# Top-k attention and a leaky MLP: the reciprocal one round later, scores before the split, weight loads from ScalarE, last chunks merged

## The chip, the core and the metric

The kernel runs on one core of a Trainium2 chip. A core has five engines with a queue each: TensorE (PE, matrix products, with PEld for its weight loads), VectorE (DVE), ScalarE (ACT), GpSimd (POOL) and SyncE (SP), which here gives out nearly all transfers. The metric is device time in microseconds, the median of several runs; lower is better.

## The reference

For 8 batches and 8 heads, 576 queries look at 576 keys of 64 elements. Of each row of scores the 32 largest are kept, a softmax is taken over them, and the values are weighed. The result, 4608 tokens of 512, goes through an MLP with a leaky activation.

```python
scores = scale * np.matmul(q, k.transpose(0, 1, 3, 2))
kth = np.partition(scores, -top_k, axis=-1)[..., -top_k:-top_k + 1]
mask = scores >= kth
scores = np.where(mask, scores, -1000000000.0)
scores = scores - np.max(scores, axis=-1, keepdims=True)
attn = np.exp(scores)
attn = attn / (np.sum(attn, axis=-1, keepdims=True) + 1e-09)
return np.matmul(attn, v).astype(np.float32)
# x = that, as 4608 x 512
h = x @ w_in                       # 512 x 2048
g = np.maximum(0.01 * h, h)
return (g @ w_out).astype(np.float32)
```

The MLP weights arrive as 64-bit floats, which the kernel turns into 32-bit ones by itself.

## The kernel before

The work is cut into 144 units, each 128 query rows of two heads. A software pipeline handles one unit per step: in step s VectorE finds the top 32 of unit s in four rounds of eight, GpSimd masks unit s-1, ScalarE exponentiates and normalizes unit s-2 and splits it into 16-bit halves for a transpose by DMA, and in every second step TensorE makes the scores of two units ahead and weighs the values of two units behind. Between these parts lie seven portions of MLP work. The engines' queues get the instructions in this order:

```python
for s in range(len(steps) + LAG + 1):
    cur, old = unit(s), unit(s - 1)
    older, oldest, new = unit(s - 2), unit(s - LAG), ()
    ...                              # every second step: new = two units ahead
    picks = top_k(cur) if cur else iter(())
    budget = slot_budget(s)

    def slot(n):
        next(picks, None)            # one top-k round
        if s in gap and n:
            convert()                # in steps 4 to 9: weights instead
    slot(0)
    if old:
        mask(old, 0); mask(old, 1)
    if older:
        exponents(older, 0); exponents(older, 1)
        sums(older)
    mlp_steps(budget)
    mlp_steps(budget)
    slot(1)
    if older:
        reciprocals(older)
    mlp_steps(budget)
    if older:
        normalize(older, 0); normalize(older, 1)
    slot(2)
    mlp_steps(budget)
    if older:
        transpose(older)
    mlp_steps(budget)
    slot(3)
    for u in new[:1]:
        scores(u)
    if s % 2 == 0:
        for u in (unit(s - LAG - 1), oldest):
            if u: weigh_values(u)
    for u in new[1:]:
        scores(u)
    mlp_steps(budget)
    mlp_steps(budget)
    ...
```

The parts that the change touches:

```python
def scores(u):                       # one PSUM buffer for both heads (psc0, psc1)
    ps = [ps_sc.tile([P, 2, 512], F32, name=f"psc{i}") for i in range(2)]
    ...                              # matmuls
    for i in range(2):
        nc.scalar.copy(u.s[i]..., ps[i][:, :, 0:HS])

def sums(u):
    nc.scalar.activation(u.ze, u.z, AF.Copy, bias=1e-9, scale=1.0)
def reciprocals(u):
    nc.vector.reciprocal(u.rz, u.ze)
def normalize(u, i):
    nc.scalar.activation(u.s[i], u.s[i], AF.Copy, bias=0.0, scale=u.rz[:, i:i + 1])

def transpose(u):
    for h in range(2):
        split = work.tile([P, 2 * S], U16, name="split", bufs=2)
        nc.scalar.copy(split, pairs[:, :, h])
        nc.sync.dma_start(apart[:, h, :], split)
    nc.sync.dma_start_transpose(out=u.wT..., in_=apart...)
```

The weights come in 16 chunks of 1 MB as 64-bit words, into three buffers (`raws`). In each slot 1 to 3 of the steps 4 to 9 (`gap`), the conversion begun two slots ago is finished on VectorE, the next is begun, and another load is given out:

```python
def convert_weights(dst, raw, on_vector):
    nc.vector.tensor_scalar(ex, hi, ...)          # begin: exponent and mantissa
    nc.vector.tensor_scalar(man, hi, ...)
    if on_vector:                                 # even chunks, counted from 0
        nc.vector.tensor_scalar(ex, ex, ...)
        nc.scalar.activation(ex, ex, ...)
    else:                                         # odd chunks
        nc.scalar.activation(exf, ex, ...)        # three on ScalarE
        ...
    nc.scalar.activation(frac, lo, ...)           # frac lies in raw
    yield
    nc.vector.scalar_tensor_tensor(out=dst, in0=man, ..., in1=frac, ...)   # finish
    nc.vector.scalar_tensor_tensor(out=ex, in0=hi, ...)                    # last to read raw
    nc.vector.tensor_tensor(dst, dst, exf, ALU.mult)

def convert():
    if len(converting) == 2 or not raw_chunks:
        for c in converting[:1]:
            next(converting.pop(0), None)
    if raw_chunks:
        begun[0] += 1
        converting.append(convert_weights(*raw_chunks.pop(0), on_vector=begun[0] % 2 == 1))
        next(converting[-1])
    fetch_weights()
```

The MLP takes tokens in chunks, numbered from 0. A chunk can begin once the values of all its tokens are weighed; its work is spread evenly over the steps until the next chunk is ready. Two chunks of 128 tokens, sixteen of 256 and two of 128 make the 4608.

```python
def mlp(ch):
    n = CHUNKS[ch]
    for f in range(NFC):                          # 16
        for c in range(HP):                       # 4
            nc.tensor.matmul(ph[:, 0:n], w_in[c][...], x[c][:, 0:n], ...)
            ...
        nc.scalar.activation(gT[f][:, 0:n], ph[:, 0:n], AF.Prelu, alpha=SLOPE)
        ...
    for r0 in range(0, n, P):
        for f in range(NFC):
            nc.tensor.matmul(pz[0:m, 0:DMODEL], gT[f][:, r0:r0 + m], w_out..., ...)
            ...
        nc.scalar.copy(o_sb[0:m], pz[0:m, 0:DMODEL])
        nc.sync.dma_start(out[...], o_sb[0:m])

def slot_budget(s):
    after = [at for at, _ in ready_at if at >= s]
    until = gap[-1] if s in gap else after[0] if after else s
    return backlog[0] / ((until + 1 - s) * SLOTS)
```

Of the kernel before, what the change touches and what calls it, by code (L numbers as in the profile page):

```python
# [17 lines left out]
def kernel(  # L18
# [13 lines left out]
    nc = tc.nc  # L32
# [13 lines left out]
    WCH = 1024  # L46
    LEFT = S % P
    assert D == 64 and S == 576 and HP == 4 and B % 2 == 0 and LEFT == 64
    CHUNKS = [128] * 2 + [256] * 16 + [128] * 2
    assert sum(CHUNKS) == B * S  # L50
    CHMAX = max(CHUNKS)
    LOADED, LOADED_V = 5, 5
# [31 lines left out]
            yield (w_out[f // 4][:, f % 4:f % 4 + 2, :],  # L84
                   moe_w_out[f * P:(f + 2) * P, :].rearrange("(g p) n -> p g n", g=2))

    def load_weights(dst, src):

        if src.dtype == F32:
            nc.sync.dma_start(dst, src)  # L90
            return None
        raw = raws.tile([P, WCH, 2], U32, name="raw")
        to = raw.rearrange("p n w -> p (n w)")
        if len(src.shape) == 3:
            dst = dst.rearrange("p g n -> p (g n)")
            to = to.rearrange("p (g n) -> p g n", g=2)
        nc.sync.dma_start(to, src)
        return dst, raw

    def convert_weights(dst, raw, on_vector):  # L100
# [29 lines left out]
    def load_qk(pi):  # L130
        qt = loads.tile([P, S], F32, name="qt")
        kt = loads.tile([P, S], F32, name="kt")
        nc.sync.dma_start(qt, qT[pi])
        nc.sync.dma_start(kt, kT[pi])
        qk_of[pi] = qt, kt

    def load_v(pi):
        v_of[pi] = loads.tile([P, NKC, 2, D], F32, name="vt", bufs=LOADED_V)
        nc.sync.dma_start(v_of[pi], vk[pi])
# [28 lines left out]
    def scores(u):  # L168
        ps = [ps_sc.tile([P, 2, 512], F32, name=f"psc{i}") for i in range(2)]
        for n in range(0, len(u.parts), 2):  # L170
            for half in range(2):
                for i, pi, side, r0 in u.parts[n:n + 2]:
                    qt, kt = qk_of[pi]
                    d = slice(side * D, (side + 1) * D)
                    nc.tensor.matmul(  # L175
                        ps[i][r0:r0 + u.rows, half, 0:HS],
                        qt[d, u.q0:u.q0 + u.rows],
                        kt[d, half * HS:(half + 1) * HS],
                        start=True, stop=True,
                    )  # L180
        u.both = work.tile([P, 2, S], F32, name="s_sb", bufs=5)
        u.s = [u.both[:, i, :] for i in range(2)]
        for i in range(2):
            nc.scalar.copy(u.s[i].rearrange("p (h n) -> p h n", h=2), ps[i][:, :, 0:HS])  # L184

    def top_k(u):

        u.tops = small.tile([P, 2, ROUNDS, 8], F32, name="tops")
        rest = [work.tile([P, S], F32, name=f"rest{i}", bufs=1) for i in range(2)]
        src = u.s  # L190
        for r in range(ROUNDS):
            for i in range(2):
                nc.vector.max(out=u.tops[:, i, r, :], in_=src[i])  # L193
            if r + 1 < ROUNDS:
                for i in range(2):
                    nc.vector.match_replace(out=rest[i], in_to_replace=u.tops[:, i, r, :],  # L196
                                            in_values=src[i], imm_value=LOWEST)
                src = rest
            yield
# [42 lines left out]
    def x_at(token):  # L242

        c = 0
        while token >= CHUNKS[c]:
            token -= CHUNKS[c]
            c += 1
# [21 lines left out]
    def mlp(ch):  # L269

        n = CHUNKS[ch]
        t0 = sum(CHUNKS[:ch])
        x = x_of[ch]
        for f in range(NFC):
            ph = ps_ml.tile([P, 512], F32, name="ph", tag="ml")
            for c in range(HP):
                nc.tensor.matmul(  # L277
                    ph[:, 0:n], w_in[c][:, f * P:(f + 1) * P], x[c][:, 0:n],
                    start=(c == 0), stop=(c == HP - 1),
                )  # L280
                if c == 1:
                    yield 2 * max(n, 225)
            nc.scalar.activation(gT[f][:, 0:n], ph[:, 0:n], AF.Prelu, alpha=SLOPE)  # L283
            yield 2 * max(n, 225)
        for r0 in range(0, n, P):
            m = min(P, n - r0)
            pz = ps_ml.tile([P, 512], F32, name="pz", tag="ml")
            for f in range(NFC):
                nc.tensor.matmul(  # L289
                    pz[0:m, 0:DMODEL], gT[f][:, r0:r0 + m], w_out[f // 4][:, f % 4, :],  # L290
                    start=(f == 0), stop=(f == NFC - 1),
                )
                if f % 2 and f + 1 < NFC:
                    yield 2 * DMODEL
            o_sb = work.tile([P, DMODEL], F32, name="o_sb", bufs=1)
            nc.scalar.copy(o_sb[0:m], pz[0:m, 0:DMODEL])  # L296
            nc.sync.dma_start(out[t0 + r0:t0 + r0 + m, :], o_sb[0:m])
            yield 2 * DMODEL
# [8 lines left out]
    def mlp_steps(budget):  # L307
        owed[0] += budget
        while owed[0] > 0:
            if running[0] is None:  # L310
                if not ready:
                    owed[0] = 0.0
                    return
                running[0] = mlp(ready.pop(0))
            cost = next(running[0], None)
            if cost is None:
                running[0] = None
            else:
                owed[0] -= cost
                backlog[0] -= cost  # L320
# [14 lines left out]
    def unit(n):  # L335
        return steps[n] if 0 <= n < len(steps) else None
# [25 lines left out]

    chunks, raw_chunks = weight_chunks(), []

    def fetch_weights():
        chunk = next(chunks, None)
        got = load_weights(*chunk) if chunk else None
        if got:
            raw_chunks.append(got)

# [6 lines that stand above are left out]
            begun[0] += 1  # L377
            converting.append(convert_weights(*raw_chunks.pop(0), on_vector=begun[0] % 2 == 1))
            next(converting[-1])
        fetch_weights()  # L380

    with tc.manual_schedule():
        last = {p: n for n, u in enumerate(steps) if u for p in u.pairs}
        for p in range(HP):
            load_qk(p)
            if p < 2:
                scores(units[p])
        for _ in range(3):
            fetch_weights()
        for p in range(HP):  # L390
            load_v(p)

        def load_more(s):

            for of, load, n, lag in ((qk_of, load_qk, LOADED, -2), (v_of, load_v, LOADED_V, LAG + 1)):
                while len(of) < NPAIR and (len(of) < n or last[len(of) - n] + lag <= s):
                    load(len(of))
# [4 lines that stand above are left out]
            if s % 2 == 0 and s not in gap:  # L402
                ahead = units if s < FIRST else steps
                new = ahead[s + 2:s + 4]
# [4 lines that stand above are left out]
                next(picks, None)  # L409
                if s in gap and n:  # L410
                    convert()

            slot(0)
            if old:
                mask(old, 0)
                mask(old, 1)
            if older:
                exponents(older, 0)
                exponents(older, 1)
                sums(older)  # L420
            mlp_steps(budget)
            mlp_steps(budget)
            slot(1)
            if older:
                reciprocals(older)
            mlp_steps(budget)
            if older:
                normalize(older, 0)
                normalize(older, 1)
            slot(2)  # L430
            mlp_steps(budget)
            if older:
                transpose(older)
            mlp_steps(budget)
            slot(3)
            for u in new[:1]:
                scores(u)
            if s % 2 == 0:
                for u in (unit(s - LAG - 1), oldest):
                    if u:  # L440
                        weigh_values(u)
# [4 lines that stand above are left out]
            attended(s)  # L446
            if s >= gap[-1]:
                load_more(s)
        mlp_steps(1e9)
# [53 lines left out]
```

## Time and profile before

The median of 3 runs is 1656.01 us (1655.76 to 1659.07); the profiled execution spans 1656.4 us.

| stretch (us) | what happens | VectorE busy | TensorE busy | ScalarE busy |
|---|---|---|---|---|
| 45 to 142 | weights are converted | 86.88 | 39.09 | 66.36 |
| 142 to 290 | top-k; few tokens for the MLP yet | 144.94 | 93.16 | 90.64 |
| 290 to 410 | steady state begins | 111.90 | 114.11 | 86.20 |
| 410 to 1520 | steady state | 1057.47 | 1052.45 | 796.31 |
| 1520 to 1593 | last top-k rounds | 48.90 | 71.00 | 40.00 |
| 1593 to 1656 | last values and MLP | 1.28 | 57.49 | 20.07 |

In the profile's lines, a group or instruction is named by line of the kernel, engine and operation, with output and input. Line 193 is the maximum of a top-k round, 196 its replacement, 221 the reciprocal, 224 the normalization, 233 the split, 184 the copy of scores out of PSUM, 175 the score matmuls, 257 the weighing of values, 277 and 289 the two MLP products, 283 and 296 their ScalarE outputs, 212 the exponentials, 217 the sum, 97 a weight load, and 108 to 124 the conversion. "Idle before" is the time in which the engine stood in front of an instruction, and the name behind the arrow is what ended it.

### The profile page before, as it was taken

The numbers are of one execution on the slowest core, as the hardware profiler recorded it, in microseconds if no ns is written. First come the engines' busy times: TensorE is split into PE (matmuls) and PEld (weight loads), VectorE is DVE, ScalarE is ACT, GpSimd is POOL, SyncE is SP. The second block draws the span as 40 slices with busy tenths as digits, with TensorE's granted clock in tenths as the row PEclk, the third lists the DMA queues.
The fourth block names the chain that finished last, engine by engine and source line by source line (L and its number), as shares of the span: only waits on it lengthen the run. The fifth ranks groups of instructions, "written<-read, shape, count | busy, mean of one in ns | idle before, by whom it ended". The sixth has DMA issues, their size and how long they took to land.

```text
span 1656.4 us, 24034 instructions
## 1 busy us (share of the span) xinstructions
PE 1445.8 (87%) x8192; PEld 971.4 (59%) x8192; DVE 1489.0 (90%) x3114; ACT 1117.9 (67%) x2149; POOL 1078.6 (65%) x724
## 2 busy tenths in 40 slices
PE   3145478999999999999999999999999999999999
PEld 2143364757574747575747474757575757575666
DVE  8889999899999999999999999999999999999530
ACT  3853676667676767676767676767676767776551
POOL 4203777777777677777777777777777777777530
PEclk9997578999999999999999999999999999999999
DMA  5561445544655446544654446544644455544330
GB/s 188 173 219 57 115 115 172 144 130 121 178 140 142 114 128 180 158 121 121 179 141 133 124 123 185 157 128 122 177 135 139 115 143 142 152 118 124 92 109 26
DMA packets 400314, 227.01 MB, mean 137 GB/s; under 512 B 343360, under 2 KB 343360, under 8 KB 399168
## 3 DMA queue, kind: packets, MB, share of 16 engines
q1 hardware_dynamic: 400192, 225.49, 48.1%
q8 instruction: 64, 1.05, 0.3%
q14 instruction: 58, 0.48, 0.1%
HBM read 46.14 MB, written 94.37 MB: 85 GB/s over the span
## 4 chain that ended last, share of the span: by engine, by line
DVE 48%; ACT 25%; PE 22%; issue 3%; DMA 1%; SPq 0%; DVEq 0%
DVE tops L193 24%; DVE rest L196 20%; ACT split L233 8%; PE psc L175 7%; PE ph L277 7%; PE pz L289 7%; ACT s_sb L212 6%; ACT s_sb L224 3%; ACT s_sb L184 2%; ACT gT L283 2%; ACT o_sb L296 1%; DVE rz L221 1%; ACT ze L217 1%; DVE ex L122 1%; DVE ex L108 1%
## 5 line engine op out<-in xcount | busy, mean ns | idle before, releaser
L207 POOL TENSOR_SCALAR pen<-s_sb,tops 128x576 f32<-128x576 f32 x288 | 638.5, 2217 | 389.2 <-DVE tops L193 365.3
L193 DVE MAX8 tops<-rest 128x8 f32<-128x576 f32 x864 | 607.9, 745 | 0.0
L277 PE MATMUL ph<-x,w_in 128*128 128x256 f32 (+1 forms) x2560 | 535.0, 370 | 23.3 <-ACT gT L283 19.0
L277 PEld LDWEIGHTS ph<-x,w_in 128*128 128x128 f32 x2560 | 460.5, 198 | 105.1 <-ACT gT L283 25.2
L289 PE MATMUL pz<-w_out,gT 128*128 128x512 f32 x1152 | 511.5, 600 | 1.1 <-ACT gT L283 1.1
L196 DVE MATCH_REPLACE8 rest<-tops,rest 128x576 f32<-128x576 f32 x576 | 423.2, 742 | 0.0
L209 POOL TENSOR_TENSOR s_sb<-s_sb,pen 128x576 f32<-128x576 f32 x288 | 406.5, 1411 | 24.1
L224 ACT ACTIVATE s_sb<-s_sb,rz 128x576 f32<-128x576 f32 x288 | 207.5, 767 | 260.2 <-DVE rz L221 260.0
L289 PEld LDWEIGHTS pz<-w_out,gT 128*128 128x128 f32 x1152 | 217.5, 191 | 267.7 <-issue 265.1
L175 PE MATMUL psc<-kt,qt 64*128 64x288 f32 (+1 forms) x1280 | 234.9, 460 | 114.6 <-ACT s_sb L184 110.1
L233 ACT COPY split<-s_sb 128x1152 uint16<-128x1152 uint16 x288 | 316.7, 1147 | 2.3
L175 PEld LDWEIGHTS psc<-kt,qt 64*128 64x128 f32 (+1 forms) x1280 | 129.0, 188 | 206.7 <-ACT s_sb L184 149.1
L257 PE MATMUL po<-wT,vt 128*64 128x128 f32 (+1 forms) x3200 | 184.9, 272 | 67.5 <-DMA wT<-apart 50.1
L212 ACT ACTIVATE s_sb<-s_sb,nbias 128x576 f32<-128x576 f32 x288 | 220.1, 768 | 12.6 <-POOL s_sb L209 12.6
L257 PEld LDWEIGHTS po<-wT,vt 128*64 128x64 f32 x3200 | 164.7, 141 | 100.5 <-DMA wT<-apart 38.0
L184 ACT COPY s_sb<-psc 128x576 f32<-128x576 f32 x288 | 169.5, 641 | 65.4 <-PE psc L175 65.4
L196 DVE MATCH_REPLACE8 rest<-tops,s_sb 128x576 f32<-128x576 f32 x288 | 211.6, 742 | 0.0
L193 DVE MAX8 tops<-s_sb 128x8 f32<-128x576 f32 x288 | 202.0, 743 | 6.5 <-ACT s_sb L184 6.5
L283 ACT ACTIVATE gT<-ph 128x256 f32<-128x256 f32 (+1 forms) x320 | 112.1, 353 | 82.0 <-PE ph L277 81.9
L221 DVE RECIPROCAL rz<-ze 128x2 f32<-128x2 f32 x144 | 23.1, 160 | 99.4 <-ACT ze L217 99.3
L205 POOL TENSOR_SCALAR nbias<-tops 128x2 f32<-128x2 f32 x144 | 33.4, 232 | 108.9 <-DVE tops L193 96.2
L296 ACT COPY o_sb<-pz 128x512 f32<-128x512 f32 x36 | 21.1, 586 | 71.6 <-PE pz L289 71.6
(26 smaller groups left out, 328.9 us busy)
## 6 DMA issues: line engine op xcount, KB each, us to landing
apart<-split SPq DMA_DIRECT2D x288, 288.0 KB, 2.1
vt<-in_vk_dram SPq DMA_DIRECT2D x32, 320.0 KB, 3.4
qt<-in_qT_dram SPq DMA_DIRECT2D x32, 288.0 KB, 3.2
kt<-in_kT_dram SPq DMA_DIRECT2D x32, 288.0 KB, 3.5
out_dram<-o_sb SPq DMA_DIRECT2D x36, 256.0 KB, 2.5
raw<-in_moe_w_in_dram SPq DMA_DIRECT2D x8, 1024.0 KB, 6.9
raw<-in_moe_w_out_dram SPq DMA_DIRECT2D x8, 1024.0 KB, 4.8
wT<-apart SPq DMA_TRANSPOSE x144, 4.5
```

Source lines behind the costliest of these rows:

```text
L175: nc.tensor.matmul(ps[i][r0:r0 + u.rows, half, 0:HS], qt[d, u.q0:u.q0 + u.rows], kt[d, half * HS:(half + 1) * HS], start=True, stop=True,)
L184: nc.scalar.copy(u.s[i].rearrange("p (h n) -> p h n", h=2), ps[i][:, :, 0:HS])
L193: nc.vector.max(out=u.tops[:, i, r, :], in_=src[i])
L196: nc.vector.match_replace(out=rest[i], in_to_replace=u.tops[:, i, r, :], in_values=src[i], imm_value=LOWEST)
L207: nc.gpsimd.tensor_scalar(pen, u.s[i], u.tops[:, i, ROUNDS - 1, 7:8], MASKED, ALU.is_lt, ALU.mult)
L209: nc.gpsimd.tensor_tensor(u.s[i], u.s[i], pen, ALU.add)
L212: nc.scalar.activation(u.s[i], u.s[i], AF.Exp, bias=u.nbias[:, i:i + 1], scale=SCALE, accum_out=u.z[:, i:i + 1])
L224: nc.scalar.activation(u.s[i], u.s[i], AF.Copy, bias=0.0, scale=u.rz[:, i:i + 1])
L233: nc.scalar.copy(split, pairs[:, :, h])
L257: nc.tensor.matmul(po[side * D:(side + 1) * D, o, :], vt[:, c, side, :], u.wT[:, c + side * NKC if c + 1 < NKC else c, r:r + n], start=(c ...
L277: nc.tensor.matmul(ph[:, 0:n], w_in[c][:, f * P:(f + 1) * P], x[c][:, 0:n], start=(c == 0), stop=(c == HP - 1),)
L289: nc.tensor.matmul(pz[0:m, 0:DMODEL], gT[f][:, r0:r0 + m], w_out[f // 4][:, f % 4, :], start=(f == 0), stop=(f == NFC - 1),)
```

## The change

The reciprocal goes behind the third top-k round, to wait less for the sum; the normalization follows it. The scores of the first unit of a group come ahead of the split in ScalarE's queue, so that the PSUM buffer is emptied sooner for the second. The weight loads within steps 4 to 9 are given out by ScalarE's queue in place of SyncE's, so that SyncE's other transfers don't stand behind them. The last two chunks of 128 tokens become one of 256.

```diff
-    CHUNKS = [128] * 2 + [256] * 16 + [128] * 2
+    CHUNKS = [128] * 2 + [256] * 17
 ...
-    def load_weights(dst, src):
+    def load_weights(queue, dst, src):
 ...
-        nc.sync.dma_start(to, src)
+        queue.dma_start(to, src)
 ...
-    def fetch_weights():
+    def fetch_weights(queue):
         chunk = next(chunks, None)
-        got = load_weights(*chunk) if chunk else None
+        got = load_weights(queue, *chunk) if chunk else None
 ...                                   # in convert()
-        fetch_weights()
+        fetch_weights(nc.scalar)
 ...                                   # the first three loads
-            fetch_weights()
+            fetch_weights(nc.sync)
 ...                                   # in the step
             slot(1)
+            mlp_steps(budget)
+            slot(2)
             if older:
                 reciprocals(older)
             mlp_steps(budget)
             if older:
                 normalize(older, 0)
                 normalize(older, 1)
-            slot(2)
-            mlp_steps(budget)
+            slot(3)
+            mlp_steps(budget)
+            for u in new[:1]:
+                scores(u)
             if older:
                 transpose(older)
-            mlp_steps(budget)
-            slot(3)
-            for u in new[:1]:
-                scores(u)
             if s % 2 == 0:
```

More of the change, by code (lines that the diff above doesn't have):

```diff
@@ L85, in weight_chunks @@
                    moe_w_out[f * P:(f + 2) * P, :].rearrange("(g p) n -> p g n", g=2))
-    def load_weights(dst, src):
+    def load_weights(queue, dst, src):
         if src.dtype == F32:
-            nc.sync.dma_start(dst, src)
+            queue.dma_start(dst, src)
             return None
```

## The prediction

> **What bounds the kernel now.** I read the page's busy shares first, then the long waits, then the chain that ended last, and last the order of instructions in three stretches: steady state, weight conversion and the end.
>
> ```profile
> PE 1445.8 (87%) x8192; PEld 971.4 (59%) x8192; DVE 1489.0 (90%) x3114; ACT 1117.9 (67%) x2149; POOL 1078.6 (65%) x724
> ...
> PE   3145478999999999999999999999999999999999
> ...
> DVE  8889999899999999999999999999999999999530
> ...
> L221 DVE RECIPROCAL rz<-ze 128x2 f32<-128x2 f32 x144 | 23.1, 160 | 99.4 <-ACT ze L217 99.3
> ```
>
> VectorE is the bound from the first slice to the third last, and its one real wait is in front of the reciprocal: 99.3 us, in 70 of 144 of them. TensorE is nearly as full from slice 8 on. Asked stretch by stretch, the 99.3 us lie so: none before 142 us, 3.0 from 142 to 290, 8.1 to 410, 52.5 to 1520 (54 waits, one for every second step), 24.1 from 1520 to 1593, and 11.6 after the last top-k round.
>
> The order of time on VectorE around one such wait (start, duration, instruction):
>
> ```profile
> 537.70 1.40 DVE L193 MAX8 tops<-s_sb 128x8 f32<-128x576 f32 x2
> ...
> 544.10 0.17 DVE L221 RECIPROCAL rz<-ze 128x2 f32<-128x2 f32 x1 [0.78 <-ACT ze L217]
> ...
> 548.27 1.41 DVE L193 MAX8 tops<-s_sb 128x8 f32<-128x576 f32 x2
> ```
>
> One step starts with the MAX8 pair that reads s_sb. The step above lasts 548.27 - 537.70 = 10.57 us; the one before it, whose reciprocal didn't wait, 537.70 - 528.00 = 9.70. A round of two MAX8 and two replacements is 2.77 us, the fourth has no replacement: 3 x 2.77 + 1.32 + 0.07 = 9.70. So a pair of steps is 19.4 us of work and takes 20.3 to 20.5.
>
> The chain that ended last says what the reciprocal waits for:
>
> ```profile
> 535.20 2.21 ACT split L233 x2
> 537.40 0.55 ACT s_sb L184
> 537.95 0.04 issue
> 538.00 1.77 PE psc L175 x8
> 539.77 1.93 PE pz L289 x4
> 541.70 0.02 issue
> 541.72 0.59 ACT o_sb L296
> 542.31 1.53 ACT s_sb L212 x4
> ```
>
> The split of one unit delays the copy that empties the score bank, this delays TensorE's scores for the second unit of the group, this the next MLP piece, whose ScalarE output stands ahead of the exponentials, and these give the sum that the reciprocal reads.
>
> **What the Trainium skill says.** "PSUM — Partial Sum Buffer", section "Engine vs sequencer instructions": the queues of ScalarE and VectorE are strict FIFO. The trace agrees: at 544.10 VectorE stood 0.78 us with a MAX8 ready behind the reciprocal. "DMA: Bandwidth & Descriptors", section "Anatomy of one DMA — SWDGE (gpsimd) path": a semaphore wait of a DMA is made on the issuing sequencer before dispatch. The trace agrees, on SyncE's queue in the conversion stretch:
>
> ```profile
> 53.99 6.88 SPq L97 DMA_DIRECT2D raw<-in_moe_w_in_dram  x2
> ...
> 89.91 36.39 SPq L97 DMA_DIRECT2D raw<-in_moe_w_out_dram  x8
> ```
>
> The first load goes out at 53.99, as VectorE finishes its last read of chunk 0 (52.72 + 1.22 = 53.94). The same page, "Issuing engines are not separate DMA queues": another issuing engine saves only the time to initiate. No trace here shows that yet; for this change it means that the loads themselves get no faster.
>
> **The change part by part.**
>
> *Reciprocal behind round three.* It moves from 5.5 us (two rounds) to 8.3 us (three) after the step's start, so the sum may be 2.8 us later; a wait of 0.8 to 1.0 is covered. *First scores ahead of the split*: the copies of the first unit come two splits (2.2 us) earlier behind the normalization. But the normalization itself is 2.8 us later, so I check the new loops against the 19.42 us of a pair.
> ScalarE loop, from an even step's start: reciprocal 8.3, normalization to split start 1.7, first copies 1.1, split 2.2, x copies 0.45, second copies 1.1, MLP piece and o_sb about 2.3, exponentials and sum 1.8: 18.95 against a reciprocal at 9.7 + 8.3 = 18.0 if the MLP piece is serial; it mostly runs on TensorE during the copies (then 17.2). DMA loop, from one odd reciprocal to the next: reciprocal to landing of the transpose 10.6 (523.82 to 529.94 + 4.5), values 2.33, scores 1.77, MLP piece 1.93, o_sb 0.59, exponentials and sum 1.8: 19.0, under 19.42 by 0.4. TensorE per pair: scores 1.17 + 1.5, values 2.33, MLP 14.1 = 19.1, also under. So VectorE's wait should all but go, with little to spare; for jitter and for TensorE's longer pieces (3.62 instead of 1.94 us, at 560, 888, 1216) I leave 6 us of the waits. Of 3.0 + 8.1 + 52.5 = 63.6 us, 57.6 come back.
>
> *Weight loads by ScalarE.* This I expect to cost. With 3 raw buffers, the load given out after the begin of chunk k takes chunk k's own buffer, so it waits until VectorE has finished chunk k, which the code places two conversions later. In ScalarE's queue that wait stands ahead of its work for chunk k+1, and VectorE's finish of k+1 needs that work. Today ScalarE runs ahead, and conversion takes 46.2 to 141.4 = 95.2 us, of which
>
> ```profile
> 76.30 0.69 DVE L108 TENSOR_SCALAR ex<-raw 128x1024 uint32<-128x1024 uint32 x1 [4.17 <-DMA raw<-in_moe_w_in_dram]
> ...
> 95.43 0.69 DVE L108 TENSOR_SCALAR ex<-raw 128x1024 uint32<-128x1024 uint32 x1 [3.98 <-DMA raw<-in_moe_w_out_dram]
> ```
>
> are 8.2 us behind late loads. New period per chunk: from VectorE's last read of raw (1.25 us before its finish ends) issue 0.5, hops 0.1, ScalarE work 4.33 (odd chunks; 52.14 to 56.47) or 2.0 (even; 48.82 to 50.81), then the finish 3.64: from finish to finish 7.3 or 5.0 us. Chunk 0 ends near 56.1; 7 x 7.3 + 6 x 5.0 = 81 to chunk 13, then 4.9 + 4.0 for the last two: 146. ScalarE's other work, now serial with this (two normalizations 2.9, two splits 4.4, two exponentials 3.6, x copies 0.4, prelus and waits for TensorE some 5, less where VectorE waits anyway), adds about 15: 161, or 20 us more than 141.4.
>
> *Last chunks of 256.* TensorE takes 0.112 us a matmul at 128 columns and 0.221 at 256 (128 in 14.34, 56 in 12.37), so a merged chunk saves no work: 56.3 us in all. What changes is where it lies. Now the budget sets chunk 17 (56 us) into four steps, 14.1 us of MLP a step against VectorE's 9.7; TensorE runs late and so do the reciprocals:
>
> ```profile
> 1573.43 0.17 DVE L221 RECIPROCAL rz<-ze 128x2 f32<-128x2 f32 x1 [4.15 <-ACT ze L217]
> ...
> 1589.69 0.17 DVE L221 RECIPROCAL rz<-ze 128x2 f32<-128x2 f32 x1 [6.47 <-ACT ze L217]
> ```
>
> After it the same work lies in eight steps, 7.1 us each, and the 24.1 us of waits go. In return the last chunk, 56.3 instead of 28.1 us, can only begin after the last values. From the end of the last top-k: chunk 17 and the values in the three steps left take TensorE about 30 us, then 56.3, then output 4.1: 90. Now it is 1656.4 - 1593.9 = 62.5. So this part gives 24.1 and takes about 28: -4 us.
>
> *Sum.* Top-k ends at 1593.9 - 87.7 (all waits before it) + 6 (left over) + 20 (conversion) = 1532; + 90 = 1622, as near 1622 beside the median.
>
> **The rivals.** (a) ScalarE's late normalization becomes the wait: the loops above have 0.4 to 0.8 us to spare; 0.5 us more latency in every pair is 0.5 x 65 = 33 us, and the result 1650. For it: three loops within 2% of the pair. Against: the parts were measured with their stalls in them. (b) Conversion costs nothing: were the loads' wait no block on ScalarE, the 8.2 us would come back and the time be about 1594. For it: ScalarE is busy only 66.4 of 97 us in that stretch. Against: the code's order, and a strict queue. (c) TensorE becomes the bound: at 95% already in 410 to 1520 (1052 of 1110), its 19.1 us a pair could be 19.6, which makes 10 us more. (d) The tail costs nothing, if the chunk's merging hides in other work; I see none after the last values.
>
> **Range and chances.** Steady state 57.6 (30 to 63), conversion -20 (-10 to -28), tail -4 (-12 to +3): predicted 1622, eight in ten between 1604 and 1642. 2% faster begins at about 1623, in the middle of this. Faster by over 2%: 0.47; within 2%: 0.50; slower by over 2%: 0.03.
>
> **What would show it.** Right: the wait of the reciprocal for ze under 10 us in all, steps of 9.7 us between 300 and 1500; in the conversion stretch new VectorE waits of 2 to 3 us for ScalarE's raw on the odd chunks, ending near 160; a last MLP stretch of 56 us on TensorE. Wrong: reciprocal waits that stay above 30 us, or a wait of TensorE for wT in every pair (rival a); conversion ending at 141 or before (b); VectorE waiting for scores (c).

## The result and the profile after

The changed kernel takes 1630.89 us (median; 1628.82 to 1638.48) against 1656.11; the ratio is 0.985, 95% interval 0.982 to 0.989. The profiled execution spans 1628.0 us. The page of the changed kernel, busy shares and slices:

```profile
PE 1425.9 (88%) x8064; PEld 954.1 (59%) x8064; DVE 1483.8 (91%) x3114; ACT 1107.9 (68%) x2133; POOL 1079.3 (66%) x724
...
PE   4125546899999998999999999999999999999998
...
DVE  8777999999999999999999999999999999999700
```

VectorE's slices are now full for the whole of the steady state, but slices 1 to 3 (counted from 0), the weight conversion, fell from 8 and 9 tenths to 7: something was given back there. The long waits (engine, line and waiting tile, what ended the wait; us in total, times, longest):

```profile
PEld po L257 <- DMA wT<-apart: 77.5, 46, 7.4
...
DVE rz L221 <- ACT ze L217: 30.5, 9, 12.1
...
DVE w_out L120 <- ACT raw L118: 16.2, 6, 6.3
DVE w_in L120 <- ACT raw L118: 15.3, 7, 4.1
```

The reciprocal's wait fell from 99.3 us in 70 places to 30.5 in 9, of which 12.1 + 4.2 lie behind the last top-k round. In its place VectorE waits 31.5 us for ScalarE's half of the conversion (1.0 before), and TensorE's weight loads more often for the transposed attention weights (77.5 us in 46 places, 38.0 in 13 before). In steady state, VectorE's order of time:

```profile
603.66 0.14 DVE L221 RECIPROCAL rz<-ze 128x2 f32<-128x2 f32 x1
605.05 1.39 DVE L193 MAX8 tops<-s_sb 128x8 f32<-128x576 f32 x2
...
613.36 0.14 DVE L221 RECIPROCAL rz<-ze 128x2 f32<-128x2 f32 x1
614.75 1.39 DVE L193 MAX8 tops<-s_sb 128x8 f32<-128x576 f32 x2
```

A step is 614.75 - 605.05 = 9.70 us, as is every step without a wait, where every second was some 10.57. Now the conversion, ScalarE first (ACTq is a transfer given out by its queue):

```profile
56.65 0.38 ACTq L97 DMA_DIRECT2D raw<-in_moe_w_in_dram  x1
57.09 1.15 ACT L115 ACTIVATE ex<-ex,ends 128x1024 f32<-128x1024 uint32 x1 [4.11 <-issue]
...
60.41 1.08 ACT L118 ACTIVATE raw<-raw 128x1024 f32<-128x1024 uint32 x1
63.97 0.34 ACTq L97 DMA_DIRECT2D raw<-in_moe_w_in_dram  x1
```

and VectorE beside it:

```profile
54.16 2.42 DVE L122 SCALAR_TENSOR_TENSOR ex<-raw,ex 128x1024 uint32<-128x1024 uint32 x1
...
61.53 1.23 DVE L120 SCALAR_TENSOR_TENSOR w_in<-w_in,raw 128x1024 f32<-128x1024 uint32 x1 [1.76 <-ACT raw L118]
...
165.86 1.23 DVE L124 TENSOR_TENSOR w_out<-w_out,ex 128x1024 f32<-128x1024 f32 x1
```

VectorE's last read of chunk 0's buffer ends at 54.16 + 2.42 = 56.58, the load goes out at 56.65, and only behind it ScalarE begins its work for chunk 1, having stood idle 4.11 us. ScalarE's work for chunk 1 ends at 61.49 and VectorE's finish of chunk 1 begins at 61.53. The conversion ends at 167.1, 25.6 us later than before (141.5). The end of the run, on TensorE:

```profile
1564.49 2.40 PE L257 MATMUL po<-wT,vt 128*64 128x128 f32 x40
1566.82 1.98 PE L289 MATMUL pz<-w_out,gT 128*128 128x512 f32 x4
1568.64 27.79 PE L277 MATMUL ph<-x,w_in 128*128 128x256 f32 x128
1596.27 27.63 PE L289 MATMUL pz<-w_out,gT 128*128 128x512 f32 x64
```

VectorE's last top-k round ends at 1538.3; 26 us later the last values are weighed, and the merged chunk alone takes 1568.6 to 1623.9. From the last round to the end are 89.7 us, against 62.5 before.

### The profile page after: what moved, and what is told of

It is laid out like the page before. It is cut to its first block, busy times and chain, and to the rows that moved or that the text cites. A ratio compares the mean times of both kernels' runs of the same rounds, so it can differ in the third digit from the quotient of the medians.

```text
span 1628.0 us, 23759 instructions
## 1 busy us (share of the span) xinstructions
PE 1425.9 (88%) x8064; PEld 954.1 (59%) x8064; DVE 1483.8 (91%) x3114; ACT 1107.9 (68%) x2133; POOL 1079.3 (66%) x724
## 4 chain that ended last, share of the span: by engine, by line
DVE 57%; PE 25%; DMA 6%; ACT 3%; issue 1%; SPq 0%; ACTq 0%
DVE tops L193 31%; DVE rest L196 25%; PE pz L289 10%; PE ph L277 10%; DMA wT<-apart 4%; PE psc L175 3%; PE po L257 3%; DMA apart<-split 1%; ACT split L233 1%; ACT s_sb L212 0%; DVE rz L221 0%; ACT s_sb L224 0%; ACT raw L118 0%; DMA vt<-in_vk_dram 0%; SPq L236 0%
## 5 line engine op out<-in xcount | busy, mean ns | idle before, releaser
L277 PE MATMUL ph<-x,w_in 128*128 128x256 f32 (+1 forms) x2432 | 526.2, 377 | 30.4 <-ACT gT L283 27.5
L277 PEld LDWEIGHTS ph<-x,w_in 128*128 128x128 f32 x2432 | 449.9, 196 | 113.2 <-ACT gT L283 31.9
L257 PE MATMUL po<-wT,vt 128*64 128x128 f32 (+1 forms) x3200 | 198.3, 276 | 119.9 <-DMA wT<-apart 69.6
L175 PE MATMUL psc<-kt,qt 64*128 64x288 f32 (+1 forms) x1280 | 214.1, 465 | 45.1 <-ACT s_sb L184 39.6
L175 PEld LDWEIGHTS psc<-kt,qt 64*128 64x128 f32 (+1 forms) x1280 | 119.3, 190 | 121.9 <-ACT s_sb L184 55.7
L212 ACT ACTIVATION_READ_ACCUMULATOR s_sb<-s_sb,nbias 128x1 f32 x288 | 58.7, 204 | 0.0
```

The lines of the kernel that those rows point to most:

```text
L175: nc.tensor.matmul(ps[i][r0:r0 + u.rows, half, 0:HS], qt[d, u.q0:u.q0 + u.rows], kt[d, half * HS:(half + 1) * HS], start=True, stop=True,)
L212: nc.scalar.activation(u.s[i], u.s[i], AF.Exp, bias=u.nbias[:, i:i + 1], scale=SCALE, accum_out=u.z[:, i:i + 1])
L257: nc.tensor.matmul(po[side * D:(side + 1) * D, o, :], vt[:, c, side, :], u.wT[:, c + side * NKC if c + 1 < NKC else c, r:r + n], start=(c ...
L277: nc.tensor.matmul(ph[:, 0:n], w_in[c][:, f * P:(f + 1) * P], x[c][:, 0:n], start=(c == 0), stop=(c == HP - 1),)
```

## The experiments

Times are medians beside the kernel before on the same chip (1654 to 1657 us); ratios are to it. "Conversion ends" is the end of VectorE's last conversion instruction.

### The reciprocal's move alone

The kernel before with only this part; the split stays ahead of the first scores.

```diff
             slot(1)
+            mlp_steps(budget)
+            slot(2)
             if older:
                 reciprocals(older)
             mlp_steps(budget)
             if older:
                 normalize(older, 0); normalize(older, 1)
-            slot(2)
-            mlp_steps(budget)
+            slot(3)
             if older:
                 transpose(older)
             mlp_steps(budget)
-            slot(3)
             for u in new[:1]:
                 scores(u)
```

> The kernel before with nothing but the reciprocal behind the third round (split still ahead of the first scores). Theory of the prediction (2.8 us of slack cover waits of 0.8 to 1.0 us): the waits of steady state go, 1656 - 57 = 1600 us (1592 to 1610). Rival (the chain runs from one reciprocal to the next, 10.6 us over split, copy, scores, MLP piece, exponentials; moving both of its ends by the same 2.8 us leaves it 0.9 us longer than a step): the wait in every second step stays, 1656 us (1645 to 1665).

Measured: 1656.15 us, ratio 1.0002 (0.9994 to 1.0011). This part, named first in the change, is worth nothing. Its chain in order of time (start, us, what):

```profile
598.79 0.08 DVE rz L221
...
599.58 0.77 ACT s_sb L224
...
600.37 2.21 ACT split L233 x2
602.57 0.55 ACT s_sb L184
603.12 0.04 issue
603.16 1.77 PE psc L175 x8
604.94 1.93 PE pz L289 x4
...
606.89 0.58 ACT o_sb L296
607.47 1.53 ACT s_sb L212 x4
...
609.03 0.21 ACT ze L217
...
609.26 0.17 DVE rz L221
```

It is the chain of before, piece by piece, with a wait of 0.78 us at its end. It starts with a normalization, which the reciprocal at 598.79 released, and ends with the next reciprocal, 10.5 us later. Moving both ends by the same 2.8 us leaves its length, and a step's 9.7 us don't hold it. The rival stands.

### The scores' move alone

```diff
             slot(2)
             mlp_steps(budget)
-            if older:
-                transpose(older)
-            mlp_steps(budget)
             slot(3)
+            mlp_steps(budget)
             for u in new[:1]:
                 scores(u)
+            if older:
+                transpose(older)
```

> The kernel before with nothing but the first scores ahead of the split; the reciprocal stays behind the second round. Theory now (the chain between two reciprocals ran over split, copy and scores; with the copy ahead of the split it is 9.0 us by the parts measured, under a step's 9.7, wherever the reciprocal stands): the waits of steady state go, 1612 us (1604 to 1620). Rival (both moves are needed, the later reciprocal gives the slack): waits of 0.5 us or more stay in every second step and the time is 1630 or more.

Measured: 1605.92 us (1604.42 to 1614.08), ratio 0.971 (0.968 to 0.974): 49 us from one moved call (the split goes behind the first scores, and so behind one portion of MLP work too). ScalarE's order of time in it:

```profile
522.81 1.44 ACT L224 ACTIVATE s_sb<-s_sb,rz 128x576 f32<-128x576 f32 x2 [4.26 <-DVE rz L221]
524.15 1.16 ACT L184 COPY s_sb<-psc 128x576 f32<-128x576 f32 x2
525.20 2.21 ACT L233 COPY split<-s_sb 128x1152 uint16<-128x1152 uint16 x2
...
530.86 0.20 ACT L217 ACTIVATE ze<-z 128x2 f32<-128x2 f32 x1
...
532.51 1.44 ACT L224 ACTIVATE s_sb<-s_sb,rz 128x576 f32<-128x576 f32 x2 [1.17 <-DVE rz L221]
```

The copy stands ahead of the split, TensorE's second scores run during the split, and the sum is ready at 531.06, 1.3 us ahead of the next reciprocal (532.32). The theory of the loop holds; the rival, that the later reciprocal is needed too, does not.

### Both moves, without the other two parts

The changed kernel with SyncE's loads and the old chunks, which is before with both moves.

```diff
-    CHUNKS = [128] * 2 + [256] * 17
+    CHUNKS = [128] * 2 + [256] * 16 + [128] * 2
 ...
-        fetch_weights(nc.scalar)
+        fetch_weights(nc.sync)
```

> The kernel before with both moves in the step (reciprocal and scores), loads by SyncE and the last chunks of 128 as before. Both theories expect 1612 us (1605 to 1619), as the parts measured add up: 1630.9 - 20.1 (loads) + 1.6 (chunks). What tells them apart is its distance to the run with the scores alone: 0 (within 5 us) by the theory now, 18 us or more by the rival.

Measured: 1612.36 us (1609.18 to 1614.51). Against the scores alone, 6.4 us more: a little over the 5 that I had allowed, with ranges that overlap. A pair on one chip, further down, takes this up again.

### Weight loads by SyncE again

```diff
-        fetch_weights(nc.scalar)
+        fetch_weights(nc.sync)
```

> The changed kernel with the weight loads given out by SyncE again. Theory (a wait in ScalarE's queue stands ahead of its conversion work and costs about 25 us): the conversion ends near 141 us as before, not at 167, VectorE no longer waits there for ScalarE's raw, and the time is 1606 us (1598 to 1614). Rival (SyncE's transfers behind the loads matter, so the move to ScalarE pays or is even): 1631 us or more.

Measured: 1610.81 us (1606.26 to 1613.64), ratio 0.972 (0.970 to 0.974). Conversion ends at 143.7, 23.4 us earlier than in the changed kernel; the time is 20.1 lower. VectorE's waits for ScalarE's raw fall from 31.5 to 4.2 us, and it again waits twice for a load (3.4 and 4.0 us). The move to ScalarE's queue costs what it seemed to cost.

### The same queue, behind the finish

```diff
     if len(converting) == 2 or not raw_chunks:
         for c in converting[:1]:
             next(converting.pop(0), None)
+        fetch_weights(nc.scalar)
     if raw_chunks:
         ...
         next(converting[-1])
-    fetch_weights(nc.scalar)
```

> The changed kernel, weight loads still by ScalarE, but each given out behind the finish of the chunk whose buffer it takes, so behind ScalarE's work on the next chunk and not ahead of it. Theory (it is the place of the wait in the queue that costs): conversion ends at 135 to 142 us, the time is 1604 us (1596 to 1612). Rival (it costs to give out transfers from ScalarE at all, or the loads come too late): conversion still ends at 155 or later and the time is 1620 or more.

Measured: 1610.83 us (1604.63 to 1612.67), again 20.1 less than the changed kernel. Waits for ScalarE's raw fall from 31.5 to 2.0 us with the transfers still in ScalarE's queue: it is the place of the wait that costs. Conversion ends at 147.0, not at 142, since VectorE now waits for loads:

```profile
DVE ex L108 <- DMA raw<-in_moe_w_out_dram: 10.5, 2, 5.9
...
DVE ex L108 <- DMA raw<-in_moe_w_in_dram: 2.7, 1, 2.7
```

So the rival has a small share: a load behind ScalarE's other work can also go out too late.

### Loads by GpSimd

```diff
-        fetch_weights(nc.scalar)
+        fetch_weights(nc.gpsimd)
```

> The changed kernel with the weight loads given out by GpSimd, which has no work of its own in the steps of the conversion once the last mask is made. Theory (only what stands behind the waiting load in its queue loses): neither ScalarE nor SyncE's transposes wait, conversion ends at 134 to 141 us and the time is 1605 us (1597 to 1613). Rival (a load given out only as its buffer comes free lands too late from any queue, or GpSimd is slow to give it out): conversion ends at 145 or later and the time is 1612 or more.

Measured: 1607.98 us (1607.62 to 1608.18), ratio 0.971 (0.970 to 0.973). Conversion ends at 140.9. GpSimd's order of time:

```profile
53.20 1.69 POOL L209 TENSOR_TENSOR s_sb<-s_sb,pen 128x576 f32<-128x576 f32 x1
56.61 0.77 POOL L97 DMA_DIRECT2D raw<-in_moe_w_in_dram  x1 [1.72 <-DVE ex L122]
62.00 0.57 POOL L97 DMA_DIRECT2D raw<-in_moe_w_in_dram  x1 [4.62 <-DVE ex L122]
```

It stands idle ahead of every load, and nothing of use stands behind. Late loads cost VectorE 1.9 us in all, against 13.2 and 7.4 in the two runs above; its waits for ScalarE's raw are 6.9 us. The theory holds: the wait is harmless in a queue that has nothing else to do.

### The old last chunks

```diff
-    CHUNKS = [128] * 2 + [256] * 17
+    CHUNKS = [128] * 2 + [256] * 16 + [128] * 2
```

> The changed kernel with the last chunks of 128 tokens again. Theory (TensorE's MLP work is the same, only its place differs; what crowds four steps is given back by a shorter end): 1625 us (1619 to 1634), with waits of VectorE for the sum of 10 to 25 us before the last top-k round and about 70 us from that round to the end instead of 90. Rival (the merging was a gain of its own): 1640 us or more.

Measured: 1632.49 us (1626.55 to 1634.89) against 1630.89 of the changed kernel, ratio to before 0.986 (0.984 to 0.988): no difference that these runs show. What moved is seen in VectorE's reciprocals:

```profile
1507.94 0.17 DVE L221 RECIPROCAL rz<-ze 128x2 f32<-128x2 f32 x1 [3.01 <-ACT ze L217]
1526.63 0.17 DVE L221 RECIPROCAL rz<-ze 128x2 f32<-128x2 f32 x1 [8.89 <-ACT ze L217]
1540.58 0.17 DVE L221 RECIPROCAL rz<-ze 128x2 f32<-128x2 f32 x1 [4.16 <-ACT ze L217]
1556.84 0.17 DVE L221 RECIPROCAL rz<-ze 128x2 f32<-128x2 f32 x1 [6.47 <-ACT ze L217]
```

22.5 us of waits in the last steps; the last round ends at 1558.3, 20 us later than with the merged chunk, and from there to the end are 66.4 us, 23 fewer. TensorE has the same products to make and is nearly full in either end (84.3 of the last 91 us in the changed kernel, 83.5 here).

### No loads of q, k and v

One of the last waits of steady state, 0.80 us at 1011.06, comes in this chain of the changed kernel:

```profile
998.11 6.08 DMA wT<-apart
1004.19 0.04 issue
1004.23 1.31 PE po L257 x20
1005.54 1.19 PE psc L175 x16
1006.73 1.93 PE pz L289 x4
...
1011.06 0.17 DVE rz L221
```

SyncE's queue gave out loads of q and k right behind that transpose, at 1000.71 to 1002.24, and the transpose took 6.08 us to land, where the median is 4.6. To see whether the loads are the cause, later pairs read the first four again; this leaves out 28 pairs of 896 KB, 25.7 MB (the expectation says 27), and the output is of other data.

```diff
-                    load(len(of))
+                    of[len(of)] = of[len(of) % HP]
```

> The changed kernel with no loads of q, k and v after the first four pairs; later pairs read the first four again, so this leaves out 27 or more MB of loads and the output is of other data. Theory (the 11 to 13 us of reciprocal waits left in steady state come where a transpose lands late beside such loads): waits of the reciprocal before the last top-k round under 3 us besides the one in the conversion and those of the last steps, time lower by 8 to 14 us: 1620. Rival (the loop over the transpose is just too long now and then): waits and time as in the changed kernel, 1628 to 1634.

Measured: 1617.90 us, 13.0 less than the changed kernel. The reciprocal's wait between 410 and 1500 us, first of the changed kernel:

```profile
DVE rz L221 <- ACT ze L217: 11.1, 5, 3.7
```

and without the loads:

```profile
DVE rz L221 <- ACT ze L217: 0.4, 1, 0.4
```

The loads are the cause: without them 1.2 us of such waits are left from 142 us to the last steps, where the changed kernel has 12.6, and the last round ends at 1526.1, 12.2 us earlier. But the way that the theory gave, a transpose that lands late beside loads, is wrong. From 410 to 1500 us this line of the transposes is the same in both runs:

```profile
DMA to landing us min/median/max: 4.3/4.6/6.2
```

In either run eight of them take 5.5 us or more; without the loads these cost VectorE 0.4 us. Of the changed kernel's five waits there, only two follow a long landing (2.50 us at 893.75, behind 5.4 us, and the 0.80 above). The longest, 3.73 us, doesn't:

```profile
643.10 4.36 DMA wT<-apart
...
647.50 1.92 PE po L257 x20
...
655.97 0.17 DVE rz L221
```

This transpose landed in 4.36 us, but it was given out 13.1 us after the one before. The two writes of the split that it needs, given out at 636.12 behind four loads of q and k, took 5.9 us to land, where the median is 2.1; without the loads none of this stretch took over 4.3. The wait of 1.79 us at 1362.20 follows writes of 4.5 us behind four such loads; the chain of the last one, 2.25 us at 716.53, runs over a load of v. At 636.12 SyncE's queue held the first write up by some 0.4 us, an estimate from the end of the split's first half, near 635.7; the rest came in landing. That speaks for the transfers' sharing more than for the queue, but no run separates the two.

### The parts that gain, together

The changed kernel with loads by GpSimd and the reciprocal behind round two, with merged and with old chunks.

```diff
-        fetch_weights(nc.scalar)
+        fetch_weights(nc.gpsimd)
 ...
             slot(1)
-            mlp_steps(budget)
-            slot(2)
             if older:
                 reciprocals(older)
             ...
+            slot(2)
+            mlp_steps(budget)
             slot(3)
```

> The changed kernel with the weight loads by GpSimd and the reciprocal back behind the second round: what the runs before left as gain, without the two parts that gained nothing. Theory (the reciprocal's place is worth nothing, the loads' queue is): 1605 us (1599 to 1610), between the run with GpSimd (1608) and 5 us under it. Rival (the later reciprocal gave slack after all): 1613 or more.

> The same with the last chunks of 128 tokens. Theory (the end is TensorE's, and the merging only moves its work): within 4 us of the other, 1605 (1599 to 1610). Rival (one of the two ends is worth more once the step doesn't wait): a difference of 6 us or more.

Measured: 1599.51 us (1596.19 to 1602.53), ratio 0.966 (0.964 to 0.968), and 1599.62 with the old chunks. Conversion ends at 137.0 and 137.9. Both are faster than the kernel before and the changed kernel, and the two ends are again alike.

For the reciprocal's place, late and early were then run side by side with the loads by GpSimd and merged chunks. Early differs from late by:

```diff
             slot(1)
-            mlp_steps(budget)
-            slot(2)
             if older:
                 reciprocals(older)
             ...
+            slot(2)
+            mlp_steps(budget)
             slot(3)
```

> The changed kernel with the weight loads by GpSimd, reciprocal behind the third round, measured again beside the next one on one chip. If the later place costs time of its own (two comparisons before hint at 6 to 8 us): 1607 us, 5 us or more above the next. If it is worth nothing either way: within 3 us of it.

> The same with the reciprocal behind the second round: 1600 us if the later place costs time of its own, within 3 us of the run above if it is worth nothing.

Measured: late 1604.12 us (1598.65 to 1611.09), early 1601.16 (1598.40 to 1606.59): 3.0 us, at the edge of what I had set for "nothing", and ratios to before of 0.9675 and 0.9669 with intervals (0.966 to 0.969, 0.965 to 0.969) that coincide. The later place was the slower one in all three comparisons (6.4 us on top of the scores' move, 8.5 between runs with GpSimd's loads on two chips, 3.0 here), and with GpSimd's loads all late runs average 1606.0 us, all early ones 1600.6. That points to a cost of a few us; since the pair on one chip overlaps and no trace names a cause, it isn't shown. Nothing points to a gain.

## Why the prediction came out as it did

Predicted 1622, in a range of 1604 to 1642; measured 1630.9.

**Steady state: right in sum, wrong in its cause.** Of 63.6 us of waits 57.6 were to come back. What stayed is 1.5 (at 303) and 11.1 (410 to 1500), 12.6 in place of 6, so 51.0 came back. But the step "a wait of 0.8 to 1.0 is covered" by a reciprocal 2.8 us later failed: that move alone gives a ratio of 1.0002. The chain that the prediction itself quoted runs from reciprocal to reciprocal; a cycle isn't shortened by moving along with it. The prediction saw that the normalization comes 2.8 us later too, but didn't take the slack back. What shortened the chain is the scores' move, which the prediction took as the helper. The sum came out because the change makes both moves.

**Rival (a) had a share.** The loop over the transpose was put at 19.0 us of 19.42, "by 0.4". Now and then loads of q, k and v use up this slack and more: of the 12.6 us of waits, 11.4 go with them. The loop had the transpose's landing at its usual 4.5 us and no term for transfers that share with it, such as the split's writes, up to 5.9 us in place of 2.1.

**Weight loads: right, and mis-sized.** 20 us predicted, 25.6 measured at the end of conversion, of which 23.4 go when SyncE gives the loads out again, and 20.1 in the time when undone. The remaining 2.2 us stay with the other parts of the change. The mechanism is as written: from 56.58 the load, ScalarE's work and VectorE's finish stand in one line. The term for "ScalarE's other work" was low. It shows in the two longest waits for raw (5.08 and 6.28 us, at 122.8 and 146.9), where the MLP's first activations and their waits for TensorE stand between the load and ScalarE's conversion work. The waits were not 2 to 3 us on the odd chunks alone, as foretold, but 0.4 to 6.3 us on 13 of the 16.

**Last chunks: right.** 90 us from the last round to the end predicted, 89.7 measured; a part of -4 us predicted, and no difference that the runs can tell from zero. The last MLP stretch takes 55.3 us for a foretold 56.

**The sum.** The last round was to end at 1532 and ended at 1538.3: 5.6 from the conversion, 6.6 from waits left over, less 5.2 that VectorE is busy for a shorter time (1483.8 us for 1489.0). Its work is no faster: a step without a wait takes 9.70 us in both kernels. But a step with a wait of 0.78 us took 10.57, 0.87 more, so a wait costs some 0.09 us beyond its idle time (in the chain of the reciprocal's move the reciprocal adds 0.08 us without a wait, 0.17 with one). For 61 waits fewer that is an estimated 5.5 us, which the prediction left out. The run with 69 waits, the reciprocal's move alone, is busy for 1489.0 us as before; every run with the scores' move, for 1482.9 to 1484.6. The tail took the predicted 90, and the median lies 2.9 us above the profiled span.

The reciprocal's waits, 30.5 us in all, are over the 10 of the prediction's sign for "right" and just over the 30 of its sign for rival (a); 16.3 of them lie behind the last top-k round, where VectorE has no other work. Rivals (b) and (c) show no sign: conversion ends at 167.1, and VectorE waits for scores only once, at the start (7.2 us, 6.5 before).

## What to carry to other kernels

Before moving an instruction to give it slack, follow the chain back from its wait: if it begins at the same instruction one turn earlier, only a shorter chain helps, and here one call ahead of two copies did what the move could not. A transfer that waits for a buffer held up all that stood behind it in its queue, so give it to a queue with nothing to do, or put it behind the work that must not wait. A late transfer on a chain is not yet the cause of its wait: see whether it is as late where the wait is gone. Spreading the last work more evenly gained nothing here, where TensorE is nearly full to the end either way.

## What the runs showed of the hardware

A 1 MB load given out by GpSimd took 5.5 to 6.0 us to land (medians of the two weights) and 0.53 to 0.77 us to give out, against 4.9 to 5.1 and 0.33 to 0.41 from ScalarE; it still made the shorter conversion, for it waited in nobody's way. SyncE's loads in the kernel before landed in 4.8 and 6.9, so the landing doesn't follow the queue alone. A transpose landed in 4.3 to 6.2 us in steady state, with loads of q and k beside it and without. A write of the split, with a median of 2.1 us, took up to 5.9 behind four such loads. A wait of VectorE of 0.78 us made its step 0.87 us longer (10.57 for 9.70).
